# A fused kernel whose second dense layer takes 512 tokens at a time, with its output turned by 90 degrees

## The chip, the cores and the metric

The kernel runs on one core of a Trainium2 chip. Its metric is device time in microseconds (us): the median of three runs. The profile comes from one more execution, recorded by the hardware profiler.

## What is computed

Three stages follow each other on 24576 tokens of 256 features (8 batches of 3072):

```python
X = np.fft.rfft(x, axis=1)                      # along the 3072 tokens of a batch
y = np.fft.irfft(X * (filt_r + 1j * filt_i), n=3072, axis=1)
x = y.reshape(24576, 256)
h = x @ w_in1                                   # first layer, 256 -> 1024
e = exp(h - h.max(-1)); sm = e / (e.sum(-1) + 1e-9)
solu = h * sm
ln = (solu - mean(solu)) / sqrt(var(solu) + 1e-6) * g_ln
x2 = ln @ w_out1                                # 1024 -> 256
h = x2 @ w_in2                                  # second layer, 256 -> 2048
out = (h / (1 + exp(-1.702 * h))) @ w_out2      # 2048 -> 256
```

## The kernel before

The filter is a Fourier transform in two steps over groups of rows (class `Filter`); batch 0 goes first, the others two at a time in the background of the layers. The tokens of a batch are cut into 12 **pairs** of 2 x 128 tokens, 96 pairs in all.

For each pair, class `First` does the first layer: `y` (inverse step of the filter, matmuls of line 581), `hidden` (line 599, 12 matmuls of 512 columns for each half of 128 tokens), then `top`, `exp`, `weigh`, `square`, `norm` on VectorE and ScalarE, a trip through DRAM that moves blocks of 32 (`shuffle`, `gather`), `turn` (32 x 32 transposes on VectorE), and `project` (line 681). Its result `x2`, 256 features by 256 tokens, is split into a high and a low part (`x2_hi`, `x2_lo`); every matmul of this layer is done as three terms, high by high, low by high and high by low.

Class `Second` does the second layer of a pair in 8 steps `d` of two feature blocks each: `hidden` (line 731, 12 matmuls of 256 columns, weights stationary), `tanh`, `gate`, `split_hi`, `split_lo`, and `output` (line 767, 12 matmuls of 256 columns, with the gated values stationary and the weights moving, so that the tokens stand on the partitions). After step 7 `finish` (line 775) copies the sum from PSUM with a factor of one half, and `store` (line 783) writes rows of 256 floats.

The sum of a pair is one PSUM tile from a pool with a single buffer:

```python
ps_o = ps("ps_o", 1)
self.o = ps_o.tile([P, 2, D], F32, tag="o", name="o")
```

so `output(0)` of the next pair waits until `finish` has read it. Every engine works its own list strictly in order, and the lists come from one written plan: each step has a time in units of 1/16 pair (tables `FIRST`, `SECOND`, `FILTER`, `DENSE`, `EARLY`), and `sorted(plan)` is the order in which all instructions are recorded. Pair `n` of the second layer starts at unit 16 n - 2, its first layer is 16 to 31 units earlier. All DMAs are issued by SyncE (SP).

Of the kernel before, what the change touches and what calls it, by code (L numbers as in the profile page):

```python
# [29 lines left out]
P = 128  # L30

Q = 32
# [6 lines left out]
FIRST = {  # L39
    "load": -15.1,  # L40
    "y": -12.95,
    "y_lo": -12.6,
    "hidden": ((-10.68, -10.16), (-5.58, -3.51)),
    "top": (-8.9, -3.0),
    "exp": (-7.95, -2.64),
    "weigh": (-7.4, -1.86),
    "square": (-6.0, -0.24),
    "norm": (-4.6, 0.2),
    "shuffle": (-4.26, 1.81),
    "gather": (-3.0, 2.69),  # L50
    "turn": (-0.26, 5.5),
    "u_hi": (1.74, 5.79),
    "u_lo": (2.2, 6.55),
    "project": ((8.7, 10.7), (11.07, 12.51)),
    "x2_hi": 13.3,
    "x2_lo": 13.6,
}

SECOND = {
    "tanh": 0.73,  # L60
    "gate": 1.2,
    "split_hi": 2.3,
    "split_lo": 2.96,
    "output": 4.6,
    "finish": 17.02,
    "store": 20.83,
}


FILTER = {  # L70
    "slots": (-1.99, 2.65, 4.65, 14.34),
    "first": (-5.5, -1.26, 0.2, 0.28),
    "second": (-6.0, -4.09, -2.29, -0.1, 2.07, 5.39, 12.71, 13.9, 15.43),
}


DENSE = {
    "start": 16.0,
    "slots": (0.39, 4.52, 8.23, 12.4),
    "second": (-8.53, -3.17, -1.92, 0.02, 0.9, 3.5, 7.46, 9.18, 11.14),  # L80
}

EARLY = {
    "end": -34.0,
    "step1": 0.99,
# [11 lines left out]
}  # L97


# [89 lines left out]
def fft_filter_solu_gelu(  # L189
# [28 lines left out]
    ps_h = ps("ps_h", 1)  # L218
    ps_m = ps("ps_m", 3)
    ps_h2 = ps("ps_h2", 2)  # L220
# [39 lines left out]
    w4 = split_pair(K2, D, "w4")  # L260

    class Weights:


        def __init__(self, dst, src, pool, gain, k0, kn, c0, cn):
            self.hi, self.lo = (t[:, k0:k0 + kn, c0:c0 + cn] for t in dst)
            self.shape = [P, kn, cn]
            k, c = slice(k0, k0 + kn), slice(c0, c0 + cn)
            if gain is None:
# [5 lines left out]
            self.pool, self.gain, self.k0 = pool, gain, k0  # L275

        def load(self):
            pool, tag = self.pool
            self.raw = pool.tile(self.shape, U64, tag=tag, name="wst")
            for part, src in self.src:  # L280
                dma(out=self.raw[part], in_=src)
# [3 lines left out]
        def magnitude(self):  # L285
            words = self.raw.rearrange("p k n -> p (k n)").bitcast(I32).rearrange(
                "p (n t) -> p n t", t=2)
            self.low, self.high = words[:, :, 0].bitcast(U32), words[:, :, 1]
            self.n = words.shape[1]
            self.mag = p2.tile([P, self.n], I32, tag="th", name="w_mag")  # L290
            self.f = self.mag.bitcast(F32)

            nc.vector.tensor_scalar(
                out=self.mag, in0=self.high, scalar1=0x7FFFFFFF, scalar2=None, op0=ALU.bitwise_and)
            nc.vector.tensor_scalar(
                out=self.f, in0=self.f, scalar1=LEAST_HIGH_WORD, scalar2=None, op0=ALU.max)
            nc.vector.tensor_scalar(
                out=self.mag, in0=self.mag, scalar1=3, scalar2=0x3FFFFFFF,
                op0=ALU.logical_shift_left, op1=ALU.bitwise_and)

        def sign(self):

            self.top = p2.tile([P, self.n], I32, tag="gh", name="w_top")
            nc.vector.scalar_tensor_tensor(
# [3 lines left out]
        def lower(self):  # L308
            self.wt = p2.tile([P, self.n], I32, tag="gl", name="w_wt")
            nc.vector.tensor_scalar(  # L310
# [9 lines left out]
        def scale_rows(self):  # L320
            if self.gain is not None:
                for k in range(self.shape[1]):
# [10 lines left out]
    def weight_parts():  # L333
        n = 0
        for dst, src, K, N, gain in (
# [7 lines left out]
            for c in range(0, N, cn):  # L343
                for k in range(0, K, kn):
                    pool = (p2, "e" if n < EARLY["count"] else "x2")
                    n += 1
                    yield Weights(dst, src, pool, gain, k, kn, c, cn)

# [136 lines left out]
    class EarlyFilter(Filter):  # L485


        pools = {
            "gt": [(p3, "gt")] * 3 + [(p1, "ut"), (p1, "mv")], "bt": [(p3, "bt")] * 3 + [(p2, "xs")] * 2}

# [68 lines left out]

    x2_t = {}  # L560

    class First:
        def __init__(self, n):
            self.n = n
            self.h, self.e, self.v, self.e_d, self.mv, self.ut = {}, {}, {}, {}, {}, {}

# [80 lines left out]
        def shuffle(self, a):  # L647


            self.e_d[a] = dr2.tile([P // Q, Q, FF1], F32, tag="e_d", name="e_d")  # L650
            dma(out=self.e_d[a].rearrange("i t x -> (i t) x"), in_=self.e.pop(a))

        def gather(self, a):
            self.mv[a] = p1.tile([P, P // Q, FF1 * Q // P], F32, tag="mv", name="mv")
            e_d = self.e_d.pop(a).rearrange("i t (b x) -> b t i x", b=P // Q)
            for b in range(P // Q):
                dma(out=self.mv[a][b * Q:(b + 1) * Q], in_=e_d[b])

        def turn(self, a):
            self.ut[a] = p1.tile([P, K1, P], F32, tag="ut", name="ut")  # L660
            nc.vector.transpose(  # L661
                out=self.ut[a].rearrange("p k (i t) -> p k i t", t=Q),
                in_=self.mv.pop(a).rearrange("p i (k f) -> p k i f", f=Q))

# [21 lines left out]
        def x2_hi(self):  # L686
            self.x2s = p2.tile([P, 2, 2, 2 * P], F32R, tag="x2", name="x2s")
            nc.scalar.copy(out=self.x2s[:, 0], in_=self.x2)  # L688

        def x2_lo(self):  # L690
            nc.vector.tensor_tensor(self.x2s[:, 1], self.x2, self.x2s[:, 0], op=ALU.subtract)
            x2_t[self.n] = self.x2s[:, 0], self.x2s[:, 1]

# [24 lines left out]
    class Second:  # L718
        def __init__(self, n):
            self.n = n  # L720
            self.t, self.g = {}, {}

        def hidden(self, d):
            x2h, x2l = x2_t[self.n]
# [33 lines left out]
        def output(self, d):  # L758
            if d == 0:
                self.o = ps_o.tile([P, 2, D], F32, tag="o", name="o")  # L760
            gh, gl = self.g.pop(d)
            terms = [(gh, w4[0]), (gh, w4[1]), (gl, w4[0])]
            for j in range(2):
                f = 2 * d + j
                for a in range(2):
                    for m, (gg, ww) in enumerate(terms):
                        nc.tensor.matmul(  # L767
                            self.o[:, a], gg[:, j, a * P:(a + 1) * P], ww[:, f],
                            start=(f == 0 and a == 0 and m == 0),
                            stop=(f == K2 - 1 and m == 2), skip_group_check=True)  # L770

        def finish(self):
            self.ob = p1.tile([P, 2, D], F32, tag="ob", name="ob")

            nc.vector.tensor_scalar(  # L775
                out=self.ob, in0=self.o, scalar1=0.5, scalar2=None, op0=ALU.mult)

        def store(self):
            b, q = divmod(self.n, NPAIR)
            ov = out[b * S:(b + 1) * S].rearrange("(m q) d -> q m d", q=N2)  # L780
            for a in range(2):
                for k, m, n, i in segments((2 * q + a) * P, P):
                    dma(out=ov[k, m:m + n], in_=self.ob[i:i + n, a])

    def plan_second(n):
        r, o, v = 16.0 * n, Second(n), SECOND
        in_order(0.0, v["tanh"], v["gate"], v["split_hi"], v["split_lo"], v["output"])
        in_order(12.0 + v["output"], v["finish"], v["store"])
        in_order(v["finish"], 14.0 + v["output"])
        for d in range(K2 // 2):  # L790
            t = r + 2 * (d - 1)
# [3 lines left out]
        at(r + v["finish"], o.finish)  # L795
        at(r + v["store"], o.store)

    NP = B * NPAIR
    for n in range(NP):
        plan_first(n)  # L800
        plan_second(n)

# [82 lines left out]
```

## Time and profile before

| | us |
|---|---|
| median of 3 runs | 3860.95 (3858.89 to 3862.86) |
| the profiled execution, its own time | 3860.85 |
| its span in the trace | 3859.1 |
| TensorE (PE) busy | 3728.0, 97% |
| VectorE (DVE) busy | 2725.2, 71% |
| ScalarE (ACT) busy | 1996.7, 52% |
| GpSimd (POOL) busy | 767.8, 20% |

The time of the execution is 1.75 us over its span. Matmuls are pipelined and their ends are modelled, so that the busy time of PE counts as busy a short gap behind each matmul; the distance from the start of one matmul to the start of the next tells the rate.

### The profile page before, as it was taken

What the parts mean: (1) busy time and instruction counts of PE and PEld (TensorE: products, weight loads), DVE (VectorE), ACT (ScalarE), POOL (GpSimd) and SP (SyncE); (2) the same over time, 40 slices, a digit from 0 to 9 for tenths busy, and PEclk for the clock granted to TensorE, in tenths of its full rate; (3) what the DMA queues carried; (4) which work ended last, traced back from release to release, by engine and by line L of the source; (5) the groups of instructions that cost most, each with busy time, mean ns of one, the idle gap of its engine ahead of it and who ended that gap; (6) DMA issues with size and microseconds to landing.
All of it is one profiled execution on the core that took longest, in us unless ns stands there. A gap on an engine that the chain in (4) does not pass through costs nothing.

```text
span 3859.1 us, 70392 instructions
## 1 busy us (share of the span) xinstructions
PE 3728.0 (97%) x27328; PEld 3493.4 (91%) x27328; DVE 2725.2 (71%) x3729; ACT 1996.7 (52%) x3554; POOL 767.8 (20%) x1397
## 2 busy tenths in 40 slices
PE   5689999999999999999999999999999999999999
PEld 2379999999999999999999999999999999999999
DVE  8667886667777777666777777666676676666665
ACT  2255665555555555554555555555555555444444
POOL 4232321221212221121222222121111111010100
PEclk6799999999999999999999999999999999999999
DMA  7744443433333333333333333333333332222221
GB/s 225 231 140 145 145 145 103 134 107 111 109 119 109 114 109 107 107 129 105 110 109 113 108 117 106 105 113 107 98 102 106 107 102 85 77 69 83 74 77 45
DMA packets 302799, 434.95 MB, mean 113 GB/s; under 512 B 36608, under 2 KB 211840, under 8 KB 302464
## 3 DMA queue, kind: packets, MB, share of 16 engines
q1 hardware_dynamic: 302464, 430.46, 36.2%
q8 instruction: 214, 3.51, 0.4%
q14 instruction: 121, 0.99, 0.1%
HBM read 232.13 MB, written 176.16 MB: 106 GB/s over the span
## 4 chain that ended last, share of the span: by engine, by line
PE 76%; issue 7%; ACT 4%; DVE 4%; DMA 2%; POOL 2%; SPq 0%; ACTq 0%; POOLq 0%; DVEq 0%
PE o L767 23%; PE h L731 22%; PE x L681 13%; PE h L599 13%; PE f L368 3%; PE yt L581 2%; DVE gl L755 1%; ACT e L611 1%; ACT h L635 1%; DMA e_d<-e 1%; DVE ob L775 1%; POOL nmu L627 1%; DMA mv<-e_d 1%; ACT fh L362 1%; ACT gh L749 1%
## 5 line engine op out<-in xcount | busy, mean ns | idle before, releaser
L731 PE MATMUL h<-x2s,w_hi 128*128 128x256 f32 x6144 | 1119.4, 284 | 0.7 <-ACT x2s L688 0.7
L731 PEld LDWEIGHTS h<-x2s,w_hi 128*128 128x128 f32 x6144 | 912.7, 191 | 18.7 <-ACT x2s L688 0.9
L767 PE MATMUL o<-w_hi,gh 128*128 128x256 f32 x3072 | 873.6, 284 | 24.8 <-DVE ob L775 22.2
L767 PE MATMUL o<-w_hi,gl 128*128 128x256 f32 x3072 | 868.7, 283 | 1.8 <-DVE gl L755 1.8
L767 PE MATMUL o<-w_lo,gh 128*128 128x256 f32 x3072 | 868.9, 283 | 0.0
L755 DVE TENSOR_TENSOR gl<-th,gh 128x512 fp32r<-128x512 f32 x768 | 563.6, 734 | 341.6 <-ACT gh L749 341.6
L767 PEld LDWEIGHTS o<-w_hi,gh 128*128 128x128 f32 x3072 | 587.2, 191 | 51.2 <-issue 22.5
L731 PE MATMUL h<-x2s,w_lo 128*128 128x256 f32 x3072 | 618.2, 283 | 0.0
L738 ACT ACTIVATE th<-h 128x512 f32<-128x512 f32 x768 | 456.4, 594 | 307.5 <-PE h L731 300.4
L749 ACT CAST gh<-th 128x512 fp32r<-128x512 f32 x768 | 471.4, 614 | 274.2 <-DVE th L743 160.8
L681 PE MATMUL x<-u,w_hi 128*128 128x256 f32 x3072 | 600.3, 283 | 0.0
L767 PEld LDWEIGHTS o<-w_lo,gh 128*128 128x128 f32 x3072 | 587.8, 191 | 7.0
L767 PEld LDWEIGHTS o<-w_hi,gl 128*128 128x128 f32 x3072 | 587.9, 191 | 2.2 <-DVE gl L755 2.2
L743 DVE SCALAR_TENSOR_TENSOR th<-th,h 128x512 f32<-128x512 f32 x768 | 520.9, 678 | 55.2 <-ACT th L738 51.5
L681 PEld LDWEIGHTS x<-u,w_hi 128*128 128x128 f32 x3072 | 500.1, 192 | 4.4 <-DVE u L671 0.2
L731 PEld LDWEIGHTS h<-x2s,w_lo 128*128 128x128 f32 x3072 | 478.0, 191 | 0.0
L615 POOL TENSOR_SCALAR q<-se 128x1 f32<-128x1 f32 x192 | 60.3, 314 | 1962.4 <-ACT e L611 1962.3
L681 PE MATMUL x<-u,w_lo 128*128 128x256 f32 x1536 | 435.3, 283 | 0.0
L605 DVE TENSOR_REDUCE nmx<-h 128x1 f32<-128x1024 f32 x192 | 234.3, 1220 | 226.7 <-PE h L599 226.7
L668 ACT CAST u<-ut 128x1024 fp32r<-128x1024 f32 x192 | 200.9, 1047 | 229.3 <-DVE ut L661 229.3
L671 DVE TENSOR_TENSOR u<-ut,u 128x1024 fp32r<-128x1024 f32 x192 | 234.4, 1221 | 109.1 <-ACT u L668 109.1
L681 PEld LDWEIGHTS x<-u,w_lo 128*128 128x128 f32 x1536 | 295.0, 192 | 3.9
(79 smaller groups left out, 5132.2 us busy)
## 6 DMA issues: line engine op xcount, KB each, us to landing
e_d<-e SPq DMA_DIRECT2D x192, 512.0 KB, 2.9
mv<-e_d SPq DMA_DIRECT2D x768, 128.0 KB, 3.0
gt<-in_groups SPq DMA_DIRECT2D x160, 264.0 KB, 3.6
xin<-in_x SPq DMA_DIRECT2D x96, 256.0 KB, 3.0
a_d<-a SPq DMA_DIRECT2D x96, 256.0 KB, 2.1
zr<-z_d SPq DMA_DIRECT2D x96, 256.0 KB, 3.0
out<-ob SPq DMA_DIRECT2D x192, 128.0 KB, 2.4
bt<-a_d SPq DMA_DIRECT2D x96, 192.0 KB, 3.3
```

The costliest lines, as they stand in the source:

```text
L368: nc.tensor.matmul(out, w[i], x[j], start=m == 0, stop=m == 2)
L599: nc.tensor.matmul(hs, xx[:, c, a * P:(a + 1) * P], ww[:, c, f * 512:(f + 1) * 512], start=(m == 0 and c == 0), stop=(m == 2 and c == 1))
L605: nc.vector.tensor_reduce(out=nmx, in_=self.h[a], op=ALU.max, axis=AX.X, negate=True)
L668: nc.scalar.copy(out=self.u[:, 0, :, a], in_=self.ut[a])
L671: nc.vector.tensor_tensor(self.u[:, 1, :, a], self.ut.pop(a), self.u[:, 0, :, a], op=ALU.subtract)
L681: nc.tensor.matmul(self.x2[:, c], ww[:, kk, c * P:(c + 1) * P], uu[:, kk], start=(c == 0 and kk == 0 and m == 0), stop=(kk == K1 - 1 and m ...
L731: nc.tensor.matmul(t[:, j], ww[:, c, f * P:(f + 1) * P], xx[:, c], start=(m == 0 and c == 0), stop=(m == 2 and c == 1))
L738: nc.scalar.activation(out=th, in_=self.t[d], func=AF.Tanh, scale=0.851)
L743: nc.vector.scalar_tensor_tensor(out=self.g[d], in0=self.g[d], scalar=1.0, in1=self.t.pop(d), op0=ALU.add, op1=ALU.mult)
L749: nc.scalar.copy(out=gh, in_=self.g[d])
L755: nc.vector.tensor_tensor(gl, th, gh, op=ALU.subtract)
L767: nc.tensor.matmul(self.o[:, a], gg[:, j, a * P:(a + 1) * P], ww[:, f], start=(f == 0 and a == 0 and m == 0), stop=(f == K2 - 1 and m == 2 ...
```

## The change

The second layer now takes **blocks**: the first and the last pair alone, the 94 between them two at a time (47 blocks). In a block of two pairs a step works on one feature block and 512 tokens, 16 steps to the block:

- `hidden` (now line 765): 6 matmuls of 512 columns a step, not 12 of 256 on two feature blocks.
- `output` (line 804): the weights are stationary, the gated values move: 6 matmuls of 512 columns. The sum has the features on the partitions and takes two PSUM banks; the pool keeps its single buffer. The bank comes from `ps_m` (3 to 2 buffers), which holds the filter's products, `yt` and `x2`.
- `finish` (line 815): four `nc.vector.transpose` of 128 x 256 a block, which turn 32 x 32 pieces. The half is folded into `w_out2` when it is loaded, and its columns are stored in another order so that the pieces fall into place (`scale_rows`, line 332, 16 more ScalarE instructions).
- `store` (line 827): eight DMAs of 32 partitions for each pair, in runs of 64 floats, not two of 128 partitions in runs of 256 floats.
- `x2` of three pairs lies in one tile. `gather` writes back into `e` in place of a tile of its own (`mv`), the last weights are staged in three buffers rather than two, and the early filter has other buffers.
- The first block (pair 0) is spread over 32 units, the last starts at unit 1534; all tables have other numbers.

```diff
-    ps_m = ps("ps_m", 3)
+    ps_m = ps("ps_m", 2)
 FIRST
-    "square": (-6.0, -0.24),
+    "square": (-7.25, 0.3),
 SECOND
-    "finish": 17.02,
-    "store": 20.83,
+    "finish": 5.0,
+    "store": 6.2,
 Weights.scale_rows
+            if self.half:
+                f, self.f = self.f, self.top.bitcast(F32).rearrange(
+                    "p (k n) -> p k n", k=self.shape[1])
+                for k in range(self.shape[1]):
+                    nc.scalar.activation(
+                        out=self.f[:, k].rearrange("p (h a c) -> p a h c", h=2, c=Q),
+                        in_=f[:, k].rearrange("p (a h c) -> p a h c", h=2, c=Q),
+                        func=AF.Copy, scale=0.5)
+    BLOCKS = [(0,)] + [(n, n + 1) for n in range(1, NP - 1, 2)] + [(NP - 1,)]
 First.gather
-            self.mv[a] = p1.tile([P, P // Q, FF1 * Q // P], F32, tag="mv", name="mv")
+            e = self.e[a].rearrange("p (i x) -> p i x", i=P // Q)
 First.x2_hi
-            self.x2s = p2.tile([P, 2, 2, 2 * P], F32R, tag="x2", name="x2s")
+            if self.n == 0:
+                x2_t.append(p1.tile([P, 3, 2, 2, 2 * P], F32R, tag="x2", name="x2s"))
+            self.x2s = x2_t[0][:, self.n % 3]
 Second.hidden
-            for j in range(2):
-                f = 2 * d + j
+            for j in range(self.nf):
+                f = self.nf * d + j
                 for m, (ww, xx) in enumerate(terms):
                     for c in range(2):
                         nc.tensor.matmul(
-                            t[:, j], ww[:, c, f * P:(f + 1) * P], xx[:, c],
+                            self.part(t, j), ww[:, c, f * P:(f + 1) * P], xx[..., c, :],
 Second.output
-                self.o = ps_o.tile([P, 2, D], F32, tag="o", name="o")
+                self.o = ps_o.tile([P, 2, 2, 2 * P], F32, tag="o", name="o")
-            terms = [(gh, w4[0]), (gh, w4[1]), (gl, w4[0])]
+            terms = [(w4[0], gh), (w4[1], gh), (w4[0], gl)]
-                            self.o[:, a], gg[:, j, a * P:(a + 1) * P], ww[:, f],
+                            o, ww[:, f, h * P:(h + 1) * P], self.part(gg, j),
 Second.finish
-            nc.vector.tensor_scalar(
-                out=self.ob, in0=self.o, scalar1=0.5, scalar2=None, op0=ALU.mult)
+                for h in range(2):
+                    nc.vector.transpose(
+                        out=ob[:, :, h], in_=self.o[:, h, i].rearrange("p (k t) -> p k t", t=Q))
 Second.store
-                    dma(out=ov[k, m:m + n], in_=self.ob[i:i + n, a])
+                    rows = ov[2 * q + i].rearrange("(k t) (a d) -> a t k d", t=Q, a=P // Q)
+                    for a in range(P // Q):
+                        dma(out=rows[a],
+                            in_=ob[a * Q:(a + 1) * Q, i * P // Q:(i + 1) * P // Q].rearrange(
+                                "t k h d -> t k (h d)"))
```

Three places show how the instructions stand. The first is PE's list where one pair's sum ends and the next begins, in the kernel before: `o` is the sum, `h` with a number the second layer's hidden tile, `gh` and `gl` the two parts of the gated values, `w_hi` and `w_lo` of the weights; the first row is the last matmul of step 7.

```order
L767 MATMUL o<-w_hi,gl 128x256
L731 MATMUL h_9663<-x2s,w_hi 128x256 [waits DVE_49]
L731 MATMUL h_9663<-x2s,w_hi 128x256
L731 MATMUL h_9663<-x2s,w_lo 128x256 x2
L731 MATMUL h_9663<-x2s,w_hi 128x256 x4
L731 MATMUL h_9663<-x2s,w_lo 128x256 x2
L731 MATMUL h_9663<-x2s,w_hi 128x256 x2
L767 MATMUL o<-w_hi,gh 128x256 [waits DVE_49,Activation_49]
L767 MATMUL o<-w_lo,gh 128x256
```

The same place of PE's list in the changed kernel, at the end of a block; `h` without a number is the first layer's hidden tile.

```order
L804 MATMUL o<-gl,w_hi 128x512
L765 MATMUL h_7366<-x2s,w_hi 128x512 [waits DVE_49]
L765 MATMUL h_7366<-x2s,w_hi 128x512
L765 MATMUL h_7366<-x2s,w_lo 128x512 x2
L765 MATMUL h_7366<-x2s,w_hi 128x512 x2
L624 MATMUL h<-w_hi,xh 128x512 [waits Activation_49]
L624 MATMUL h<-w_hi,xh 128x512
L624 MATMUL h<-w_lo,xh 128x512 x2
L624 MATMUL h<-w_hi,xl 128x512 [waits DVE_49]
L624 MATMUL h<-w_hi,xl 128x512
L804 MATMUL o<-gh,w_hi 128x512 [waits DVE_49,PE_49,Activation_49]
L804 MATMUL o<-gh,w_lo 128x512
```

Between the last matmul into the old sum and the first into the new one PE had 12 matmuls of 256 columns; now it has 12 of 512. The second place is VectorE's list around the same end of a sum, before:

```order
L661 STREAM_TRANSPOSE ut<-mv 128x1024 [waits DMAHW2_49,DMAHW3_49,DMAHW1_49,DMAHW0_49]
L644 TENSOR_SCALAR e<-e,nmu,rs 128x1024 [waits Activation_49,Pool_49]
L755 TENSOR_TENSOR gl<-th,gh 128x512 [waits PE_49,Activation_49]
L775 TENSOR_SCALAR ob<-o 128x512 [waits PE_49]
L743 SCALAR_TENSOR_TENSOR th<-th,h_9178 128x512 [waits Activation_49]
```

and VectorE's list there in the changed kernel:

```order
L696 TENSOR_TENSOR u<-ut,u 128x8x128 [waits Activation_49]
L669 TENSOR_SCALAR e<-e,nmu,rs 128x1024 [waits Activation_49,Pool_49]
L615 TENSOR_TENSOR xl<-yt,xh 128x512 [waits Activation_49]
L815 STREAM_TRANSPOSE ob<-o 128x8x32 [waits PE_49]
L815 STREAM_TRANSPOSE ob<-o 128x8x32 x3
L789 TENSOR_TENSOR gl<-th,gh 128x512 [waits Activation_49]
L777 SCALAR_TENSOR_TENSOR th<-th,h_7315 128x512 [waits Activation_49]
```

The one copy has become four transposes, and the `gl` that the next sum needs stands behind them rather than ahead. The third place is SP's list behind a store, before (`e_d<-e` is `shuffle`, `xw<-xs` the filter's swap, DMAHW numbers are the eight counters that DMAs take in turn):

```order
L461 DMA xw<-xs 48x512 [waits DMAHW3_49]
L783 DMA out<-ob 128x256 [waits DMAHW4_49,DVE_49]
L783 DMA out<-ob 128x256
L427 DMA bt<-a_d_112 96x2x256 [waits DMAHW6_49]
L429 DMA gt<-in_groups 96x704 [waits DMAHW7_49]
L651 DMA e_d<-e 128x1024 [waits DMAHW0_49,DVE_49]
```

and SP's list at the end of a block's sixteen stores in the changed kernel:

```order
L827 DMA out<-ob 32x4x64 [waits DMAHW7_49]
L827 DMA out<-ob 32x4x64 [waits DMAHW0_49]
L827 DMA out<-ob 32x4x64 [waits DMAHW1_49]
L495 DMA z_d_117<-z 96x256 [waits DMAHW2_49,Activation_49]
L474 DMA xw<-xs 48x256 [waits DMAHW3_49,Activation_49]
L475 DMA xw<-xs 48x256 [waits DMAHW4_49]
L676 DMA e_d<-e 128x1024 [waits DMAHW5_49,DVE_49]
```

Sixteen stores in a row, once a block, stand ahead of the filter's traffic and the next `shuffle`, where two stood for each pair.

## Rows read from the trace of the kernel before

**Rows 1.** The page, its first line and the busy time of each engine.

```profile
span 3859.1 us, 70392 instructions
PE 3728.0 (97%) x27328; PEld 3493.4 (91%) x27328; DVE 2725.2 (71%) x3729; ACT 1996.7 (52%) x3554; POOL 767.8 (20%) x1397
```

**Rows 2.** Busy time by stretch: length, each engine, granted clock, DMA share, GB/s.

```profile
0.00:226.00 226.00, 146.32 (x388) 75.48 (x389) 164.90 (x262) 64.10 (x125) 91.56 (x137) 0.73 0.73 223
226.00:306.00 80.00, 77.87 (x581) 73.83 (x580) 58.85 (x81) 45.15 (x81) 20.03 (x35) 1.00 0.40 115
306.00:600.00 294.00, 286.55 (x2061) 266.53 (x2060) 237.58 (x328) 181.17 (x333) 84.87 (x123) 1.00 0.48 143
600.00:2600.00 2000.00, 1963.62 (x14577) 1859.07 (x14576) 1416.33 (x1860) 1074.13 (x1885) 401.83 (x702) 1.00 0.36 112
2600.00:3800.00 1200.00, 1199.26 (x9281) 1164.57 (x9280) 816.59 (x1159) 609.30 (x1096) 167.84 (x398) 1.00 0.29 90
3800.00:3859.00 59.00, 54.37 (x451) 53.96 (x449) 30.95 (x44) 22.84 (x38) 1.66 (x4) 1.00 0.10 32
```

**Rows 3.** Timeline of PE in the last third: start, length, instruction and count.

```profile
3318.57 0.63 PE L599 MATMUL h<-w_hi,xh 128*128 128x512 f32 x2
...
3321.32 0.40 PE L731 MATMUL h<-x2s,w_hi 128*128 128x256 f32 x2
...
3322.75 0.28 PE L767 MATMUL o<-w_hi,gh 128*128 128x256 f32 x1
...
3327.07 0.28 PE L681 MATMUL x<-u,w_hi 128*128 128x256 f32 x1
```

**Rows 4.** The chain that ended last, where one pair ends: start, length, what.

```profile
756.05 1.46 PE o L767 x12
...
757.52 1.78 DVE gl L755
759.31 0.61 DVE ob L775
...
760.05 1.67 PE o L767 x12
```

**Rows 5.** Waits of the whole run: us in total, times, longest.

```profile
PE o L767 <- DVE ob L775: 22.2, 36, 1.3
...
PE h L599 <- ACT h L635: 23.7, 44, 1.9
```

**Rows 6.** Groups of the page, second layer on PE: busy, mean ns, idle before.

```profile
L731 PE MATMUL h<-x2s,w_hi 128*128 128x256 f32 x6144 | 1119.4, 284 | 0.7 <-ACT x2s L688 0.7
...
L767 PE MATMUL o<-w_hi,gh 128*128 128x256 f32 x3072 | 873.6, 284 | 24.8 <-DVE ob L775 22.2
```

**Rows 7.** The same chain, a group of six that stands alone.

```profile
3330.11 1.39 PE h L599 x6
```

**Rows 8.** Windows of line 688 alone, once per pair: busy time and count.

```profile
300.00:2600.00 2300.00, 34.05 (x58) 1.00 0.38 116
```

**Rows 9.** Groups by line on DVE: busy, mean ns, idle before and its releasers.

```profile
L661 DVE STREAM_TRANSPOSE ut<-mv 128x1024 f32<-128x1024 f32 x192 | 237.5, 1237 | 30.4 <-DMA mv<-e_d 29.3 <-issue 0.8
L671 DVE TENSOR_TENSOR u<-ut,u 128x1024 fp32r<-128x1024 f32 x192 | 234.4, 1221 | 109.1 <-ACT u L668 109.1
...
L691 DVE TENSOR_TENSOR x2s<-x,x2s 128x512 fp32r<-128x512 f32 x96 | 66.3, 691 | 21.6 <-ACT x2s L688 21.6
...
L775 DVE TENSOR_SCALAR ob<-o 128x512 f32<-128x512 f32 x96 | 65.2, 680 | 3.6 <-PE o L767 3.5
```

**Rows 10.** Waits of SP's own queue: us in total, times, longest.

```profile
SPq L651 <- DVE e L644: 1629.1, 182, 15.2
```

**Rows 11.** Line 783, the stores: ns min/median/max of one issue, first and last start.

```profile
L783 SPq DMA_DIRECT2D out<-ob x192: 332/434/1587, 272.5 to 3856.2; - x192
...
DMA to landing us min/median/max: 1.7/2.4/4.8
```

**Rows 12.** Groups by line, the scaling of the weights on ACT.

```profile
L324 ACT ACTIVATE w_mag<-w_mag,g_sb 128x256 f32<-128x256 f32 x8 | 3.6, 500 | 12.7 <-POOL w_mag L317 12.7
```

More of the change, by code (lines that the diff above doesn't have):

```diff
@@ L39 @@
 FIRST = {
[L40 to L46, printed above, removed]
-    "square": (-6.0, -0.24),
[L48 to L55, printed above, removed]
+    "load": -18.49,
+    "y": -15.7,
+    "y_lo": -15.4,
+    "hidden": ((-13.6, -11.51), (-5.09, -3.6)),
+    "top": (-10.5, -2.4),
+    "exp": (-9.6, -1.76),
+    "weigh": (-8.86, -1.07),
+    "square": (-7.25, 0.3),
+    "norm": (-6.23, 0.53),
+    "shuffle": (-5.5, 1.2),
+    "gather": (-4.48, 1.94),
+    "turn": (-1.56, 6.83),
+    "u_hi": (-0.97, 7.3),
+    "u_lo": (-0.15, 8.0),
+    "project": ((9.4, 10.4), (11.4, 12.1)),
+    "x2_hi": 12.78,
     "x2_lo": 13.6,
@@ L59 @@
 SECOND = {
[L60 to L63, printed above, removed]
+    "tanh": 0.7,
+    "gate": 1.19,
+    "split_hi": 2.42,
+    "split_lo": 3.19,
     "output": 4.6,
-    "finish": 17.02,
-    "store": 20.83,
+    "finish": 5.0,
+    "store": 6.2,
 }
 FILTER = {
-    "slots": (-1.99, 2.65, 4.65, 14.34),
-    "first": (-5.5, -1.26, 0.2, 0.28),
-    "second": (-6.0, -4.09, -2.29, -0.1, 2.07, 5.39, 12.71, 13.9, 15.43),
+    "slots": (-0.46, 3.41, 4.65, 14.35),
+    "first": (-5.5, -2.15, 0.2, 0.29),
+    "second": (-4.91, -3.88, -2.29, -0.1, 0.66, 6.42, 12.54, 15.05, 15.71),
 }
 DENSE = {
-    "start": 16.0,
-    "slots": (0.39, 4.52, 8.23, 12.4),
-    "second": (-8.53, -3.17, -1.92, 0.02, 0.9, 3.5, 7.46, 9.18, 11.14),
+    "start": 15.65,
+    "slots": (0.77, 4.65, 8.65, 12.36),
+    "second": (-6.99, -2.67, -1.85, -0.07, 0.61, 5.46, 7.59, 10.78, 11.33),
 }
 EARLY = {
-    "end": -34.0,
+    "end": -37.0,
     "step1": 0.99,
@@ L718, in fft_filter_solu_gelu, with __init__, part @@
     class Second:
-        def __init__(self, n):
-            self.n = n
+        def __init__(self, block):
+            self.block = sorted(block, key=lambda n: n % 3)
+            self.nf = 2 // len(block)
             self.t, self.g = {}, {}
+        def part(self, t, j):
+            return t if self.nf == 1 else t[:, j]
         def hidden(self, d):
-            x2h, x2l = x2_t[self.n]
+            i, k = self.block[0] % 3, self.block[-1] % 3
+            x2 = x2_t[0][:, i:k + 1:max(k - i, 1)] if k > i else x2_t[0][:, i]
+            x2h, x2l = (x2[..., h, :, :] for h in range(2))
             t = ps_h2.tile([P, 2, 2 * P], F32, tag="h2", name="h2")
             terms = [(w3[0], x2h), (w3[1], x2h), (w3[0], x2l)]
-            for j in range(2):
-                f = 2 * d + j
+            for j in range(self.nf):
+                f = self.nf * d + j
                 for m, (ww, xx) in enumerate(terms):
@@ L775, in finish @@
-            nc.vector.tensor_scalar(
-                out=self.ob, in0=self.o, scalar1=0.5, scalar2=None, op0=ALU.mult)
-        def store(self):
[L779 to L782, printed above, removed]
-                    dma(out=ov[k, m:m + n], in_=self.ob[i:i + n, a])
-    def plan_second(n):
-        r, o, v = 16.0 * n, Second(n), SECOND
+            self.ob = []
@@ L787, in plan_second @@
+    def plan_second(block, start, spacing):
+        o, v = Second(block), SECOND
+        steps = K2 // o.nf
         in_order(0.0, v["tanh"], v["gate"], v["split_hi"], v["split_lo"], v["output"])
[L788 to L791, printed above, removed]
+        in_order(v["output"], v["finish"], v["store"])
+        in_order(v["finish"], v["output"] + 2)
+        for d in range(steps):
+            t = start + spacing * d - 2
@@ L794, in plan_second @@
                 at(t + v[step.__name__], step, d)
-        at(r + v["finish"], o.finish)
-        at(r + v["store"], o.store)
-    NP = B * NPAIR
+        end = start + spacing * (steps - 1) - 2
+        at(end + v["finish"], o.finish)
+        at(end + v["store"], o.store)
     for n in range(NP):
         plan_first(n)
-        plan_second(n)
+    for k, block in enumerate(BLOCKS):
+        plan_second(block, 32.0 * k, 4.0 if k == 0 else 2.0)
     v = EARLY
```

69 lines of the change are left out of this document (43 added, 26 removed).

## The prediction

> **What bounds the kernel now.** First the page: PE is busy 97% of the span, VectorE 71%, ScalarE 52% [rows 1]. Then the same by stretch [rows 2]. The reader is to see three regimes. Up to 226 us PE works 146 of 226 at a granted clock of 0.73 while the DMA engines are busy 0.73: loading and the first filter set the pace. From 226 to 2600 us, with the filter in the background, PE is near its limit but stops now and then: 36 us of idle time in the 2000 from 600 to 2600, at the full clock (1.00, the upper level of 2.4 GHz). From 2600 on, without that filter work, PE has no gap to speak of (1199.3 of 1200).
>
> A busy PE is not yet a PE at its rate, so the timeline comes next. In a stretch without waits, 12 first-layer matmuls of 512 columns start between 3318.57 and 3321.32: 2.75 / 12 = 0.2292 us from start to start. The 36 of 256 columns from 3322.75 to 3327.07 take 4.32 / 36 = 0.1200 each [rows 3]. Every matmul in both stretches loads its own weights. Two of 256 columns thus cost 0.2400, one of 512 costs 0.2292: 0.0108 us less for the same work. That is the core of the case, and because PE sets the pace it goes straight to the end time.
>
> Then the stops. The chain of waits shows where one pair's sum ends and the next begins: PE's last `o` group ends at 757.5, `gl` and `ob` follow on VectorE, and PE resumes `o` at 760.05 [rows 4]; of these 2.5 us PE fills 1.44 with one hidden group. The waits sum it up: 22.2 us in 36 stops for `ob`, and 23.7 in 44 for the first layer's `h`, which is free only after `square` on ScalarE [rows 5]. A matmul lasts 0.284 in the record but 0.120 in the stream [rows 3, 6], so each stop hides 0.16 more: 22.2 + 36 x 0.16 = 28 and 23.7 + 44 x 0.16 = 31, 59 us in all.
>
> **The matmuls.** Lines 731 and 767 have 9216 matmuls each (`hidden` uses `w_hi` twice, 6144 + 3072; `output` has three terms of 3072) [rows 6], 192 for each of 96 pairs. Of these, 94 pairs change: 94 x 192 / 2 = 9024 pairs of matmuls become one each. 9024 x 0.0108 = 97 us off. The low end of this term is from the one group of six that stands alone in the chain, 1.39 us [rows 7]: 0.2317 each, 0.0083 saved, 75 us. I take 97, since a long stream of groups is nearer to the twelve. The layout of `output` changes which operand is stationary, but both orders already occur: the first layer holds the tokens, `hidden` of the second the weights, and both keep their rate.
>
> The Trainium skill, in "TensorE: Matmul & The Clock Gate", section "Back-to-back issue gap", gives the gap of an isolated matmul as N / 2.4 ns plus a fixed 2.5 ns. By it one of 512 would save 2.5 ns over two of 256; an estimate from that is 23 us in place of 97. The rows above show a fixed part over four times as large, and they decide.
>
> **The wait for the sum.** 28 us over the 58 pairs from 300 to 2600 [rows 8] are 0.48 us a pair. The wait comes at each of 47 block ends now, not at every pair. VectorE does four transposes of 128 x 256 from PSUM in place of one copy of 0.68 [rows 9]. No row shows a transpose of that size or from PSUM. Below, the 1024-column one at 1.237 scaled to a quarter is 0.31; above, one could cost as much as that, 1.24. Two subtractions of 512 and 1024 columns, 0.691 and 1.221, the shorter one from PSUM, give 1.035 ns a column and 0.16 fixed [rows 9], so 0.43 for 256 columns. I take 0.43, since the long transpose costs nearly what the long subtraction does: 4 x 0.43 = 1.72, or 1.04 more than now. In return PE's list has 12 matmuls of 512 columns between the two sums, 2.75, where it had 12 of 256, 1.44: 1.31 more cover. So 0.48 + 1.04 - 1.31 = 0.21 a block, times 47 = 10 us. With no wait it is 0; with nothing covering the transposes, 47 x 1.72 = 81. Behind the transposes on VectorE stand `gl` and `gate`, and behind `gl` the same `output` on PE; that is why the upper end is not excluded.
>
> **The wait for `h`.** `square` and the `hidden` behind it are 2.16 units apart in the new plan, 0.42 before, for the first half; the second half's distance is cut from 5.56 units to 2.1. I take half of 31, 15; ends 0 and 31.
>
> **What I cost at nothing, and its cover.** The bank taken from `ps_m`: its users stand 0.85 to 4 units apart in the filter's plan, and evacuations are short; if not, the wait falls on filter matmuls and is of the order of the present `ob` stop, 0.6. The stores: 16 issues of 0.434 are 6.9 us a block on SP. SP waits 1629.1 us in 182 stops for `norm` ahead of `shuffle`, 9.0 each [rows 10, 11]: this slack covers the burst, and the filter's `xw` and `z` behind it have several units before anyone reads them. `gather` into `e`: the tile is needed again a whole pair later. The 16 scalings of weights at 0.5 us [rows 12], 8 us in the stretch where ScalarE works 64 of 226. The staging and early buffers: between -10 and +10, value 0, because that stretch is set by DMA and the first chain, which keep their order.
>
> **Start and end.** From 226 to 306 us two pairs of both layers are done; now only one pair of the second layer stands there, and its 192 x 0.12 = 23 us come at the end. If PE stays as full as it is in this stretch (77.9 of 80 [rows 2]) that is neutral. Cover gone, it costs 23. At the very end eight stores of 0.434 are issued one after the other, not two [rows 11], and two transposes stand for one copy: +3.
>
> **Sum.** 3859.1 - 97 - 59 + 10 + 15 + 3 = 3731.1 span; with the 1.75 us around it 3733. The profiled execution (3860.85) is as good as the median (3860.95), so this stands for the median too.
>
> **Rivals.**
> - *The four transposes stay uncovered* (chance 0.10): VectorE comes late because `norm`, `xl` and the transposes stand in one row there. 81 in place of 10: 3804. For it speaks that the wait exists today, against it the longer PE work in between and VectorE's 29% of idle time.
> - *The fixed cost saved is only 2.5 ns a matmul* (0.05): the 0.0108 belongs to something else that the new groups keep. 23 in place of 97: 3807. The Trainium skill's rule above says as much; the rows speak against it.
> - *The thinner first block is not filled* (0.10): the first 32 units take as long as before, being set by the first layer's chain: 3733 + 23 = 3756. For it, VectorE is at 74% in that stretch and 81% in the next [rows 2].
> - *Slower: a transpose costs the whole 1.24* (0.04). The wait is 0.48 + (4.95 - 0.68) - 1.31 = 3.44 a block, 162 in all in place of 10: 3885. It decides from 1.11 us a transpose on: there 47 x (0.48 + 4.44 - 0.68 - 1.31) = 138 eats the remaining gain of 128 and the 10 already counted.
> - *Slower: the stores hold up SP* (0.02). Four times as many pieces, each store landing at four times 2.4 = 9.6 us; eight are in flight, so a block's burst takes 19.2, 3.2 beyond the 6.9 + 9.0 of issue and slack: 47 x 3.2 = 150, 3883. The trace's longest landing is 4.8 [rows 11], and the point is 8. The Trainium skill, in "DMA: Bandwidth & Descriptors", section "Specifications", speaks for it: below 512 B a piece needs a read-modify-write, and the pieces shrink from 1 KB to 256 B; no row isolates such a store.
> - *The saving is given back elsewhere and the time stays* (0.03): 3861.
>
> **Numbers.** The forecast, 3733, has 0.66; its own range is 3700 (no waits, early -10) to 3780 (both waits as long as now, +34, and early +10). With the rivals, faster by over 0.2% is 0.66 + 0.10 + 0.05 + 0.10 = 0.91, within 0.2% 0.03, slower by over 0.2% 0.06; 0.2% is about what a measurement of this kernel can tell. For 8 in 10 the range is 3700 to 3805: it takes in the thinner block, and the uncovered transposes to their middle.
>
> **What the profile after would show.** Second-layer groups of six at 1.38 us in the chain, with PE starts 0.229 apart; about 18300 matmuls, 9024 fewer; transposes of line 815 near 0.43; waits `o <- ob` of about 10 us in at most 47 stops; SP's wait for `norm` shorter by some 4 us each second time. From 2600 us on, PE as full as now. The forecast is wrong if the groups of six take over 1.42, if PE's idle time between 600 us and the end of the filter exceeds 36 us, or if the second layer starts much later than 225 us.

## The result and the profile after

The changed kernel takes 3742.5 us (3740.7 to 3744.4, 4 runs) where the kernel before, on the same chip, takes 3860.4 (3858.9 to 3862.9, 4 runs): 0.9694 times as long, 95% interval 0.9677 to 0.9711, or 118 us less. The profiled execution has a span of 3741.6 us. The forecast was 3733, so it was 9.5 us low.

First the page of the changed kernel, the lines that answer to [rows 1]:

```profile
span 3741.6 us, 53627 instructions
PE 3633.5 (97%) x18304; PEld 3017.0 (81%) x18304; DVE 2691.7 (72%) x3825; ACT 1998.7 (53%) x3570; POOL 860.0 (23%) x1397
```

9024 matmuls are gone, as forecast. VectorE and ScalarE have about the work they had, GpSimd 92 us more of it. PE's share stays at 97%: it is still the bound. The windows of the changed kernel, in the columns of [rows 2]:

```profile
226.00:306.00 80.00, 67.82 (x416) 59.74 (x415) 52.55 (x71) 40.04 (x71) 22.09 (x36) 0.94 0.41 118
306.00:600.00 294.00, 293.52 (x1466) 242.58 (x1465) 246.94 (x351) 189.72 (x349) 93.44 (x128) 1.00 0.52 147
600.00:2600.00 2000.00, 1991.82 (x10073) 1666.56 (x10072) 1438.40 (x1995) 1118.66 (x1966) 478.41 (x734) 1.00 0.40 116
```

Two things are to be seen. Between 306 and 2600 us the idle time of PE fell from 43.8 us to 8.7. Between 226 and 306 it rose, from 2 us to 12, and the granted clock there is 0.94 in place of 1.00. The waits of PE between 306 and 2600 us say what is left of the stops of [rows 5]:

```profile
PE x L706 <- DVE u L696: 8.0, 32, 0.3
PE o L804 <- DVE ob L815: 0.5, 3, 0.2
```

The wait for `h`, 19.0 us in 39 stops in the same stretch of the kernel before, is gone, and the one for `ob` nearly so. A wait that the kernel before did not have stands in their place: `project`, the first layer's second matmul, waits for `u_lo` on VectorE. Next the timeline of PE in a stretch without the filter, where six `output` matmuls stand in a row:

```profile
3200.42 0.39 PE L804 MATMUL o<-gh,w_hi 128*128 128x512 f32 x1
...
3201.55 0.39 PE L804 MATMUL o<-gl,w_hi 128*128 128x512 f32 x1
3201.78 0.28 PE L706 MATMUL x<-u,w_hi 128*128 128x256 f32 x1
```

From 3200.42 to 3201.78 is 1.36 us for six, 0.227 each; forecast were 1.38 and 0.229. The transposes and the stores, by their lines (ns min/median/max, first and last start; then who waited, or the landing):

```profile
L815 DVE STREAM_TRANSPOSE ob<-o x192: 402/409/450, 299.5 to 3735.0; 128x256 f32<-128x256 f32 x192
...
  PE o L804: 1.7, 5
```

```profile
L827 SPq DMA_DIRECT2D out<-ob x768: 315/430/1938, 300.4 to 3738.6; - x192
...
DMA to landing us min/median/max: 1.5/1.6/3.6
```

A transpose takes 0.409 us (forecast 0.43), and PE waited for them 1.7 us in 5 stops of the whole run (forecast 10 in 47). A store, now 32 KB, a quarter of the size of before, lands in 1.6 us, sooner than the 2.4 of the larger ones in [rows 11].

**Where the 117.5 us of span lie.** `x2_hi` runs once a pair, at the border of the two layers, so its starts are milestones. By line 715 of the changed kernel, line 688 of the kernel before:

```profile
L715 ACT CAST x2s<-x x96: 587/587/587, 226.3 to 3684.9; 128x512 fp32r<-128x512 f32 x96
```

```profile
L688 ACT CAST x2s<-x x96: 585/587/587, 224.1 to 3827.8; 128x512 fp32r<-128x512 f32 x96
```

Read in the same way, with the start for pair 2 from the timeline of ScalarE, and for three experiments told below:

| kernel | start to pair 0 | pair 0 to 2 | pair 2 to 95 | pair 95 to end | span |
|---|---|---|---|---|---|
| before | 224.1 | 73.9 | 3529.8 | 31.3 | 3859.1 |
| after | 226.3 | 67.1 | 3391.5 | 56.7 | 3741.6 |
| narrow matmuls, else as after | 223.3 | 68.1 | 3471.0 | 58.1 | 3820.5 |
| before, both waits shortened | 226.0 | 73.4 | 3482.0 | 31.3 | 3812.8 |
| after, `project` behind `hidden` | 223.0 | 63.7 | 3372.4 | 56.7 | 3715.9 |

The long middle gave 138.3, the start (the first two columns) 4.6, and the end took 25.4 back. The forecast for the middle was 97 + 59 - 10 - 15 = 131, for start and end together a loss of 3.

### The profile page after: what moved, and what is told of

Read it like the earlier page. It is cut to its first block, busy times and chain, and to the rows that moved or that the text cites. A ratio compares the mean times of both kernels' runs of the same rounds, so it can differ in the third digit from the quotient of the medians.

```text
span 3741.6 us, 53627 instructions
## 1 busy us (share of the span) xinstructions
PE 3633.5 (97%) x18304; PEld 3017.0 (81%) x18304; DVE 2691.7 (72%) x3825; ACT 1998.7 (53%) x3570; POOL 860.0 (23%) x1397
## 4 chain that ended last, share of the span: by engine, by line
PE 83%; DVE 7%; DMA 3%; issue 3%; POOL 1%; ACT 1%; SPq 1%; DVEq 0%; POOLq 0%; ACTq 0%
PE h L765 24%; PE o L804 24%; PE x L706 15%; PE h L624 12%; PE f L382 5%; PE yt L606 2%; DVE e L649 1%; DVE u L696 1%; DVE th L777 1%; SPq L827 1%; DMA wst<-in_w_in 1%; POOL mt L454 1%; DVE ob L815 1%; DMA xw<-xs 1%; DMA e_d<-e 0%
## 5 line engine op out<-in xcount | busy, mean ns | idle before, releaser
L765 PE MATMUL h<-x2s,w_hi 128*128 128x512 f32 (+1 forms) x3136 | 956.5, 387 | 0.0
L765 PEld LDWEIGHTS h<-x2s,w_hi 128*128 128x128 f32 x3136 | 571.7, 189 | 107.6
L706 PE MATMUL x<-u,w_hi 128*128 128x256 f32 x3072 | 622.9, 285 | 11.6 <-DVE u L696 10.5
L804 PE MATMUL o<-gh,w_hi 128*128 128x512 f32 (+1 forms) x1568 | 615.9, 393 | 2.0 <-DVE ob L815 1.7
L804 PE MATMUL o<-gl,w_hi 128*128 128x512 f32 (+1 forms) x1568 | 607.4, 387 | 0.0
L804 PE MATMUL o<-gh,w_lo 128*128 128x512 f32 (+1 forms) x1568 | 606.6, 387 | 0.0
L765 PE MATMUL h<-x2s,w_lo 128*128 128x512 f32 (+1 forms) x1568 | 478.3, 386 | 0.0
L804 PEld LDWEIGHTS o<-gl,w_hi 128*128 128x128 f32 x1568 | 295.0, 188 | 68.9 <-DVE gl L789 9.6
L804 PEld LDWEIGHTS o<-gh,w_hi 128*128 128x128 f32 x1568 | 296.1, 189 | 63.8 <-issue 11.0
L804 PEld LDWEIGHTS o<-gh,w_lo 128*128 128x128 f32 x1568 | 296.1, 189 | 51.0
L649 DVE SCALAR_TENSOR_TENSOR e<-h,e 128x1024 f32<-128x1024 f32 x192 | 232.2, 1209 | 33.3 <-ACT e L636 20.7
```

Source lines behind the costliest of these rows:

```text
L649: nc.vector.scalar_tensor_tensor(out=e, in0=self.h[a], scalar=1.0, in1=e, op0=ALU.mult, op1=ALU.mult, accum_out=su)
L706: nc.tensor.matmul(self.x2[:, c], ww[:, kk, c * P:(c + 1) * P], uu[:, kk], start=(c == 0 and kk == 0 and m == 0), stop=(kk == K1 - 1 and m ...
L765: nc.tensor.matmul(self.part(t, j), ww[:, c, f * P:(f + 1) * P], xx[..., c, :], start=(m == 0 and c == 0), stop=(m == 2 and c == 1))
L804: nc.tensor.matmul(o, ww[:, f, h * P:(h + 1) * P], self.part(gg, j), start=(f == 0 and m == 0), stop=(f == K2 - 1 and m == 2))
```

## The experiments

The theory was that the width of the matmuls gives about 100 us and the two old waits the rest. Its rival was that the new plan and buffers give most of it, and the width only 2.5 ns a matmul. All times are given as the difference of the ratios to the kernel before times its 3861 us; each ratio has about 0.0015 on either side, so differences under some 9 us between two kernels are not told apart by it, and for these the milestones are read, each from one trace. The middle repeats well: it is 3391.5 us in the changed kernel, and 3391.7 in two made from it below (whole rows stored, `project` half a unit later). The start does not: in the changed kernel and the six below that keep its start, pair 2 starts between 291.4 and 295.0 us and pair 6 between 451.7 and 455.9.

**Narrow matmuls again.**

```diff
-    nc.tensor.matmul(o, ww[:, f, h * P:(h + 1) * P], self.part(gg, j), ...)
+    for i in range(len(self.block)):
+        gs = self.part(gg, j) if self.nf == 2 else gg[:, i]
+        nc.tensor.matmul(self.o[:, h, i], ww[:, f, h * P:(h + 1) * P], gs, ...)
```

and the same in `hidden`. 

> The changed kernel with its plan, buffers and transposes, but each 512-column matmul of both parts of the second layer is issued as two of 256 again (9024 more matmuls). If the gain is the matmuls' width: by the forecast's 0.0108 us a pair 9024 x 0.0108 = 97 more, 3840; by the 0.0122 that the merged stretch of the new trace gives (7.05 us less per six pairs), 110 more, 3852. The rival, that only 2.5 ns a matmul is fixed and the new plan and the shorter waits made the gain: 23 more, 3765.

Measured: 3822.7, ratio 0.9891 (0.9875 to 0.9908), 76 us slower than the changed kernel. The rival's 23 is out. It is also less than both figures of the theory, and its windows say why:

```profile
600.00:2600.00 2000.00, 1999.95 (x14950) 1903.30 (x14949) 1410.45 (x1951) 1103.29 (x1927) 471.27 (x719) 1.00 0.39 114
```

With narrow matmuls PE has next to no idle time here: slower matmuls give VectorE time, and the wait of `project` is not there. So the 76 are the width less what the new wait takes back; how much that is, the last experiment measures.

**Only `output` narrow**, the diff above alone. 

> As the one before, but only the output matmuls are issued as two of 256; hidden keeps 512. output holds 3 of 6 matmuls a unit, so if width alone counts, half of the other kernel's loss: 49 to 55, 3791 to 3797. If the new layout of output (weights stationary) carries more or less of the gain than hidden, the loss is clearly off half.

Measured: 3786.6, ratio 0.9801 (0.9786 to 0.9815), 41 slower, 54% of the other loss, which these intervals do not tell from half. The middles do: 3471.0 us with both narrow, 3435.5 with `output` alone narrow, and 3372.4 in the wide kernel without the wait of `project` (the last experiment); PE stands idle under 2 us from 600 to 2600 in all three. Widening `hidden` first gave 35.5, `output` after it 63.1. One reason for the uneven halves is seen in the timeline of this kernel, where a wide group of `hidden` stands between narrow ones:

```profile
3251.42 0.63 PE L765 MATMUL h<-x2s,w_hi 128*128 128x512 f32 x2
...
3252.81 0.40 PE L805 MATMUL o<-gh,w_hi 128*128 128x256 f32 x2
```

Six take 1.39 us here, as in [rows 7], and 1.36 in the changed kernel, where wide ones stand ahead: the wide ones gain a little more when their neighbours are wide too, so the half that is widened last gains more. Whether the new layout of `output` has a share besides is open: no run has `hidden` alone narrow.

**The transposes twice.**

```diff
-                for h in range(2):
+                for h in (0, 1, 0, 1):
                     nc.vector.transpose(...)
```

> The changed kernel with each block's four transposes done twice, to the same places: 4 x 0.41 = 1.64 us more of VectorE at every block end. If the forecast's formula holds (0.21 us of open wait a block, every further us of VectorE goes to PE), 47 x 1.64 = 77 more, 3820. If the cover is larger than the formula had it, under 20 more, below 3762; the wait for ob in the trace then shows how much of the 1.64 is open.

Measured: 3803.5, ratio 0.9843 (0.9829 to 0.9858), 58 slower. The wait, in the whole run:

```profile
PE o L804 <- DVE ob L815: 51.9, 47, 2.4
```

All 47 block ends stop now. The middle grows by 57.4 us, 1.22 of the 1.64 a block. If every further us of VectorE goes to PE once the cover is used up, as the formula of the forecast has it, 0.42 of VectorE's time was still covered: the formula counted 0.21 open where 0.42 was spare, 0.6 us a block too much. With one size of extra work tried, the slope itself is assumed and not shown.

**Whole rows stored.**

```diff
-                    for a in range(P // Q):
-                        dma(out=rows[a], in_=ob[a * Q:(a + 1) * Q, ...].rearrange("t k h d -> t k (h d)"))
+                    dma(out=ov[2 * q + i], in_=ob[:, ...].rearrange("p k h d -> p (k h d)"))
```

> The changed kernel with two stores a pair of 128 partitions and 1 KB runs in place of eight with 256 B runs; it writes the turned pieces as they lie, so the values of the output stand in another order. If SP's slack covers the stores, as the forecast has it: no more than the tail, 0 to 3 us faster, 3739 to 3742. The rival, that small stores hold up SP or the DMA engines in the stream: more than 10 faster, below 3732.

Measured: 3740.9, ratio 0.9682 (0.9668 to 0.9697); the interval overlaps that of the changed kernel. The middle is 3391.7 us against 3391.5, the end 53.7 against 56.7: the forecast's 3 us of tail, and nothing in the stream. The Trainium skill, in "DMA: Bandwidth & Descriptors", section "Specifications", says that pieces below 512 B pay a read-modify-write; no run here isolates that. The small stores landed in 1.6 us, and the time of the stream did not depend on them.

**Two sums in the kernel before.**

```diff
-    ps_m = ps("ps_m", 3)
+    ps_m = ps("ps_m", 2)
-    ps_o = ps("ps_o", 1)
+    ps_o = ps("ps_o", 2)
```

> The kernel before with the buffers of PSUM shared out as in the change: two for the sum, two in place of three for the filter; nothing else. If the wait for the sum costs what the forecast took it for, 28 us less: 3833. The rival: the missing third buffer or the next stop takes it back, and the time stays within 5 us of 3860 or rises.

Measured: 3853.1, ratio 0.9977 (0.9967 to 0.9987), 9 faster than before in place of 28. Its waits:

```profile
PE h L599 <- ACT h L635: 39.8, 46, 2.0
...
PE o L767 <- DVE gl L755: 5.5, 17, 1.1
PE f L368 <- DVE pr L454: 3.0, 3, 1.2
```

The wait for `ob` is gone, and the wait for `h` took most of it: 39.8 us where [rows 5] has 23.7. The last line is a new one, the filter waiting for one of its two banks.

**`square` planned late in the changed kernel.**

```diff
-    "square": (-7.25, 0.3),
-    "norm": (-6.23, 0.53),
-    "shuffle": (-5.5, 1.2),
+    "square": (-5.55, 0.3),
+    "norm": (-5.3, 0.53),
+    "shuffle": (-5.0, 1.2),
```

> The changed kernel with square, norm and shuffle of the first half planned right ahead of the hidden that reuses their buffer (square at -5.55 in place of -7.25, hidden at -5.09). If the wait for h costs what the forecast took it for, 15 to 31 us come back: 3757 to 3773. If ScalarE's queue and not the distance set that wait, no change: 3740 to 3746.

Measured: 3747.1, ratio 0.9704 (0.969 to 0.9719), no difference outside the intervals; the middle is 3392.9 us, 1.4 longer, and the wait for `h` between 306 and 2600 is 0.5 us in one stop. So the distance from `square` to the `hidden` behind it, on which the forecast rested, is not what made that wait. In the kernel before, ScalarE itself stood idle ahead of `square` (line 635) for `nmu`, which follows `weigh`, as the line below from its source view says; in the changed kernel this is 3.8 us in 4 times:

```profile
  POOL nmu L627: 116.7, 144
```

What the change lengthened is the run from `hidden`'s first half to its second, from 5.1 to 8.5 units, in which `top`, `exp`, `weigh` and `square` must all fit; a later experiment tests this.

**The first layer's new times in the kernel before**, with two sums and with one. The first layer's table becomes that of the change, but for `load`:

```diff
-    "load": -15.1, "y": -12.95, "hidden": ((-10.68, -10.16), (-5.58, -3.51)),
-    "top": (-8.9, -3.0), ..., "project": ((8.7, 10.7), (11.07, 12.51)), "x2_hi": 13.3,
+    "load": -17.0, "y": -15.7, "hidden": ((-13.6, -11.51), (-5.09, -3.6)),
+    "top": (-10.5, -2.4), ..., "project": ((9.4, 10.4), (11.4, 12.1)), "x2_hi": 12.78,
```

> The kernel before with two sums in PSUM and with the change's times for the first layer (hidden's first half two to three units earlier, so that top, exp, weigh and square have 6.4 units in place of 4.6 before hidden's second half wants their buffer); load stands at -17, since the filter isn't done with the tile earlier. Narrow matmuls, old stores. If the two waits share one cost, so that removing one alone feeds the other, both gone give the forecast's 59: 3802, and more than the sum of the two kernels that remove one each. The rival, that the waits are worth little and the changed plan of the rest gave the difference: within 15 of 3853.

> As the one before, but with one sum in PSUM and three buffers for the filter, as the kernel before has them: only the wait for h is taken away. If the wait for h costs the forecast's 31 by itself: 3830. If the sum's wait takes over what is gained here, as the wait for h grew from 19.0 to 33.6 us where the sum's was taken away: 5 to 20, 3842 to 3857.

Measured: 3945.3, ratio 1.0214 (1.02 to 1.0228), and 3938.4, ratio 1.0195 (1.0181 to 1.0209). Both are slower than before, which neither theory expected. The waits of the first of them:

```profile
PE yt L581 <- DMA zr<-z_d: 41.5, 16, 5.8
...
PE f L368 <- DVE pr L454: 21.0, 15, 2.5
PE h L599 <- DVE xl L590: 18.6, 35, 1.3
```

The wait of `hidden` for `square` is gone, but `y`, planned 2.75 units earlier, now waits for the filter's output `z` to be read back, since the filter's times were left as they were. The two kernels settle nothing on the question; they show that these times cannot be borrowed without the filter's.

**Less moved: 0.9 units.** Two sums, and only the chain from `hidden`'s first half to `square` earlier:

```diff
-    "load": -15.1, "y": -12.95, "y_lo": -12.6,
-    "hidden": ((-10.68, -10.16), ...), "top": (-8.9, ...),
-    "exp": (-7.95, ...), "weigh": (-7.4, ...), "square": (-6.0, ...),
+    "load": -15.6, "y": -13.7, "y_lo": -13.35,
+    "hidden": ((-11.55, -11.05), ...), "top": (-9.8, ...),
+    "exp": (-8.85, ...), "weigh": (-8.3, ...), "square": (-6.8, ...),
```

> The kernel before with two sums in PSUM, and hidden's first half with top, exp, weigh and square 0.8 to 0.9 units (about 2.2 us) earlier, load and y with them; everything else, the filter's times too, as before. The longest stop for h was 1.6 us with two sums. If the two waits are one cost that only falls when both are taken away, the forecast's 59 come off nearly whole: 3802 to 3815. If another stop takes their place again, as the wait for h did when the sum's was taken away alone: 3840 to 3855.

Measured: 3813.7, ratio 0.9875 (0.9859 to 0.9891), 48 faster than before. The waits that are left of the old ones and the two new ones:

```profile
PE yt L581 <- DMA zr<-z_d: 10.2, 10, 1.7
...
PE f L368 <- DVE pr L454: 8.2, 8, 1.4
...
PE h L599 <- ACT h L635: 1.1, 1, 1.1
```

The second sum alone gave 9; with the earlier chain it is 48, with 18 us of new stops in it. Here the run-up to `square` and its distance from the next `hidden` both grew; with the late `square` above, which had the short distance and no wait, this points to the run-up. The two old waits share cost: with the sum's taken away alone, PE reached `h` earlier and waited there. What the earlier chain gives with a single sum was not run in a kernel free of other stops, so whether the sum's wait would take over in the same way is not shown.

**Three single pairs at the start.**

```diff
-    BLOCKS = [(0,)] + [(n, n + 1) for n in range(1, NP - 1, 2)] + [(NP - 1,)]
+    BLOCKS = [(0,), (1,), (2,)] + [(n, n + 1) for n in range(3, NP - 1, 2)] + [(NP - 1,)]
...
-        plan_second(block, 32.0 * k, 4.0 if k == 0 else 2.0)
+        if k < 3:
+            plan_second(block, 64.0 / 3 * k, 8.0 / 3)
+        else:
+            plan_second(block, 32.0 * (k - 1), 2.0)
```

> The changed kernel with the first 64 units shared by three single pairs (0, 1 and 2) in place of one single pair and one block of two. If the thinner first block leaves PE unfilled (16 of the forecast's 23 us, read from the start of pairs 0 and 2 in the new trace), a second-layer unit every 2.67 in place of 4 units fills part of it: 5 to 13 us faster, 3729 to 3737, less 2.3 for the pairs kept narrow. If the first layer's chain sets that stretch whatever PE is given, the time is 3742 to 3745.

Measured: 3745.0, ratio 0.9699 (0.9685 to 0.9714): no gain. Its windows:

```profile
226.00:306.00 80.00, 72.69 (x504) 65.83 (x503) 56.05 (x78) 44.85 (x79) 27.31 (x37) 0.98 0.41 121
306.00:600.00 294.00, 287.77 (x1546) 241.75 (x1545) 242.92 (x342) 185.58 (x339) 99.08 (x126) 0.99 0.52 145
```

PE is fuller by 4.9 us up to 306 and emptier by 5.8 up to 600: pair 2 starts at 291.7 in place of 293.4, pair 6 at 453.5 in place of 452.3, both within the spread given above. Second-layer work handed to PE there does not bring the stream forward; what holds it in that stretch is elsewhere.

**`project` later**, first by half a unit, then by more.

```diff
-    "project": ((9.4, 10.4), (11.4, 12.1)),
+    "project": ((9.9, 10.8), (11.6, 12.1)),
```

> The changed kernel with project's four parts planned 0.5, 0.4, 0.2 and 0 units later, so that VectorE's u_lo has 1.9 units in place of 1.4 before it. If the new wait of project for u costs what the trace gives it, 8.0 + 32 x 0.16 = 13 us in the stretch from 600 to 2600: those come back, about 3729. If it only shows a lag that the next stop takes over: within 4 of 3742.

Measured: 3746.0, ratio 0.9698 (0.9684 to 0.9711), no difference, and its wait stands at 8.1 us in 32 stops. The order of PE's instructions shows that the test missed its mark: the first part of `project` still stood behind the same `output` group. So its first part was moved to 10.2:

```diff
-    "project": ((9.4, 10.4), (11.4, 12.1)),
+    "project": ((10.2, 10.8), (11.6, 12.1)),
```

> The changed kernel with project's first part planned at 10.2 in place of 9.4: one hidden group of six (1.36 us) now stands ahead of it on PE. The kernel with 9.9 had left the first part at its place in PE's list, between the same two groups, and so left its wait for u as it was. If that wait is what it shows, 8.0 + 32 x 0.16 = 13 us in the stretch from 600 to 2600, it goes and the time is about 3729 to 3733. If VectorE as a whole is behind there and the next reader stops in its place: within 4 of 3742.

Measured: 3720.1 (3717.7 to 3723.4), ratio 0.9634 (0.9619 to 0.9648), 23 us faster than the changed kernel and 141 faster than the one before. It is the fastest of the kernels run here. PE in the long stretch, and who waits for `u_lo` in the whole run:

```profile
600.00:2600.00 2000.00, 1999.79 (x10163) 1678.83 (x10161) 1449.02 (x2017) 1125.45 (x1988) 493.65 (x745) 1.00 0.40 117
```

```profile
  PEld x L706: 1.8, 3
  PE x L706: 1.2, 2
```

In the changed kernel the same two lines read:

```profile
  PEld x L706: 18.8, 42
  PE x L706: 10.5, 34
```

The middle fell by 19.1 us. The weight loads' wait fell by 17.0, which is near it; PE's own fell by 9.3, and the 13 worked out from PE's idle time was too small.

## Why the prediction was right, and where its numbers were off

The direction and the mechanism were right; the point forecast was low by 10.5 us of span. By its own terms:

- **The matmuls, 97.** Of two kernels whose PE has no gap from 600 to 2600, narrow and wide, the middle is 3471.0 and 3372.4: 98.6 us for 93 x 96 = 8928 pairs of matmuls, 0.0110 each. The forecast's 0.0108, read from two short stretches of the trace before, holds. It is a mean: a group of six wide ones takes 1.39 us behind narrow matmuls (0.0083 saved for each) and 1.36 behind wide ones (0.0133), and the twelve of [rows 3] were one of each. That the new stream's mix comes so near the same mean was not worked out, and is in part luck. The rival of 2.5 ns does not hold; the Trainium skill, in "TensorE: Matmul & The Clock Gate", section "Back-to-back issue gap", gives this figure for an isolated matmul, and the stream here decides otherwise.
- **The old waits, 59.** From the kernel before to the narrow one the middle falls by 58.8 us at equal matmuls, and PE's idle time from 306 to 2600 us from 43.8 to 0.1. The size was right for both together. Taken apart as 28 and 31 it was wrong: the second sum alone gave 9, with 3.0 us of new waits for the filter's bank in it. What the wait for `h` is worth alone stays open.
- **The new waits, 10 + 15.** Here the steps failed, and that the sum came out near is luck. The wait for the sum is 1.7 us in place of 10, since VectorE had some 0.4 us to spare where the formula had a lack of 0.21; the rival of this term, the uncovered transposes, is out. The wait for `h` is nothing in place of 15, because it did not hang on the distance that the forecast looked at. And a wait of 19 us that it did not price came: `u_lo` to `project`, 2.15 units apart in the plan before, 1.40 in the new one. The forecast measured two distances of the plan and passed over this third, which was cut too.
- **The start, 0.** This is the step that put the number low, under "Start and end". The first stretches lost 2.3 + 16 = 18 us: pair 0 to 2 took 67.1 us where 73.9 less 23 would be 51 had PE stayed full. The rival of the thinner first block had most of its 23 us; it came true beside the forecast rather than in place of it. Not all of this is waiting: from 226 to 306 us PE is idle for 10 us more than before, and its granted clock is 0.94 on the mean where it was 1.00, which is another 5 us. The clock is 0.84 from 236 to 246 us and 0.68 from 246 to 256, between the levels of 1.2 and 2.4 GHz, and 1.00 again from 256; PE had been busy 7.1 of the ten us before 236, against 8.9 in the kernel before. The waits of PE from 226 to 300 us show whom it waited for:

```profile
PE h L624 <- ACT xh L611: 3.1, 2, 2.1
PE x L706 <- DVE u L696: 2.5, 2, 1.3
PE h L624 <- DVE xl L615: 2.2, 2, 1.4
```

  All are steps of the first layer's own chain. Three single pairs put second-layer work into the hole, with the clock at 0.98, and pair 2 came no earlier than in the spread of the others. That the chain as such sets this stretch is argued from these waits, and no run shortened it. That the fastest kernel has 63.7 us here, below all others, says only that `project`'s place has a part in it.
- **The tail, +23 and +3.** 25.4 measured; the 3 us of the eight stores were seen by themselves.
- **What was costed at nothing.** The stores cost the stream nothing. The bank taken from `ps_m` cost it nothing either: from 226 us on no wait for such a bank is among PE's. In the first 226 us it does show, which the forecast had no row for: `a` (line 430) empties the bank that the first filter step (line 426) wants next.

```profile
PE f L426 <- DMA xin<-in_x: 23.2, 9, 6.6
PE f L426 <- ACT a L430: 15.3, 9, 3.3
```

  Before, the two were 38.6 and 6.3 us; with the bank moved and nothing else (two sums in the kernel before) they are 29.3 and 15.9, the same sum, and `x2` of pair 0 comes 0.7 us later. So there the wait for the bank stands in the place of a wait for the load. SP's wait for `norm`, as in [rows 10], is 919.0 / 173 = 5.3 us now, 9.0 before, 3.6 less on the mean where the forecast had 4 less at every second one. Sixteen stores in place of four a block account for 5 us of the 15 that four such waits lost; where the rest went, in the plan's new times for instance, was not followed. The slack was still enough.

```profile
SPq L676 <- DVE e L669: 919.0, 173, 13.6
```

In sum: the middle gave 98.6 + 58.8 - 19.1 = 138.3 where 131 was forecast, and the start took 18 where 0 was. The three parts add up by construction, as each is the difference of two middles in the table above.

## What to carry to other kernels

Where one engine is full, price a wider instruction by start-to-start times of both widths in the trace before: two short stretches gave 97 us for 9024 pairs of matmuls, and 8928 of them measured 98.6. Its waits for two buffers may share one cost: the 59 us of both came off together, the removal of the first alone gave 9. When a table of times is replaced, list every producer and consumer whose distance became shorter, not only those that waited before: the one that was passed over cost 19 us, and moving a single group behind another gave it back.

## What the runs showed that was not expected

- A transpose of 128 x 256 from PSUM took 402 to 450 ns, a third of the 1237 ns of the 128 x 1024 one from SBUF in [rows 9].
- Six wide matmuls took 1.36 us behind wide ones and 1.39 behind narrow ones, 0.227 and 0.232 each.
- PE's idle time understated the stop at `project`: once it was gone, PE's own waits were 9.3 us less, its weight loads' 17.0, and the middle 19.1.
- Moving one PSUM bank from the filter to the sum turned a wait of the first stretch from the load to the bank without lengthening it: 38.6 + 6.3 us before, 29.3 + 15.9 after.
